# RWKV-style recurrence and two MoE layers on one core: prefix products by scans on chip, 64-row product pairs, and a new order

## The chip, the cores and the metric

The kernel runs on one core of one Trainium2 chip. The metric is the device time of one execution in microseconds. Of the kernel before there are three runs (1366.8, 1375.52 and 1378.17 us, median 1375.52) and one profiled execution.

## The reference

For each of 4 batches and 8 heads a 40x40 state is carried over 768 steps; then two MoE layers without routing follow (really two dense feed-forward layers of 3072 tokens, 320 -> 2048 -> 320):

```
for t in range(768):                       # per batch, head; all 40 wide
    y[t]  = r[t] @ state
    Sa    = state @ a[t]
    state = state * w[t] - outer(Sa, b[t])   # w in 0.85..0.95
    state = state + outer(v[t], k[t])
x = y as (3072 tokens, 320)
h = x @ w_in;  x = (h * sigmoid(h)) @ w_out          # layer 1
h = x @ w_in2; out = max(0.01*h, h) @ w_out2         # layer 2
```

The weights come as 64-bit floats and are turned into 32-bit ones on the chip.

## The kernel before, in words

The recurrence is cut into 12 chunks of 64 steps. A chunk c has two halves of 16 heads, and the program counts them as x = 0..23 (x = 2c + half). In a chunk everything is matrix products, after each step's keys and queries are scaled by the running product of w (P) or by its reciprocal (Q).

**Start.** `prefix(g)` (L626) computes P for a group of four chunks, in rows of steps: 14 products on `scratch`, a clamp, two reductions into `pmm`, eight reciprocals of 320 elements, and it writes P and Q to four DRAM tensors, as rows (`pd`, `qd`) and transposed (`ptd`, `qtd`). Group 0 is on VectorE, groups 1 and 2 multiply on GpSimd. In the same time 40 pieces of the first layer's weights are decoded (`w1_piece`, L883) in slots of `carved` and `scratch`.

**Attention.** `pre(x)` (L675) loads P and Q, forms SA = a*P, transposes K and b (`kr`), multiplies them by Q (`kbt`), and multiplies `kbt` with SA on TensorE in two groups of four 128x128x128 products (`bank<-sa,kbt`; two matmul records each). VectorE masks a part back into SA, ScalarE copies a part that goes to DRAM (`s2d`). `solve(c)` (L726) loads it back spread over 128 partitions (`ilm`), runs a 32-step substitution of 62 operations on GpSimd (`ilt`, `ily`), and writes `yd`. `chain(x)` (L753) loads that as `yt`, computes the states' part (`tv,sa`), two solves (`carved,yt` and `uv,s`), the state update (`uv,kb`), the product of uv with r (`carved,uvt`, two groups of four 128x128x128 products against RB, a block-diagonal copy of r), and the outputs (`carved` with TT, then `kb,carved`), which times P give `xt`, 128 tokens of layer-1 input. The ring `sa` has four buffers, and `pre` and `solve` of chunk c+1 are recorded ahead of the chains of chunk c.

**MoE.** Every two chains complete a block of 256 tokens, for which `moe_block` (L488) multiplies in the float32-rounded format with high and low parts, 16 steps f of 14 matmuls: eight of `xs` with the first weights and six of `gs` with the second. Between them ScalarE takes SiLU and VectorE the low part of `gs`. Blocks 0 to 10 of layer 1 run between attention work (phase 1). Block 11 and the 12 blocks of layer 2 run behind it (phase 2). In phase 1 the second layer's weights are decoded too, in 20 pieces, and kept in DRAM (`w2d`).

**What sets the order.** Every operation is recorded and then ordered by `Plan.run` (L242), a greedy list scheduler: at each step it takes, on the engine that can start first, the task with the lowest due time. The due times come from the table DUE (L339), one row for each kind of work with offsets for the first few uses; `cost` (L122) holds what it assumes of durations. It also hands out PSUM banks (four of group `t` for attention, two `h` and two `o` for the MoE). All recorded operations therefore show line L370 in the profile (L386 in the changed kernel). All transfers are issued by SyncE.

Of the kernel before, what the change touches and what calls it, by code (L numbers as in the profile page):

```python
# [58 lines left out]
class Plan:  # L59
# [5 lines left out]
    QUEUE, LAND = 800.0, 1350.0  # L65

    def __init__(self, nc, groups):
        self.nc, self.groups = nc, groups
        self.tasks, self.log, self.cur, self.done, self.since = [], {}, None, {}, 0.0
        self.busy = {k: [0.0] * len(v) for k, v in groups.items()}  # L70
        self.free = dict.fromkeys(self.HOP, 0.0)
        self.dma, self.port = 0.0, {"vector": 0.0, "gpsimd": 0.0}
        self.win, self.work, self.warm, self.mode = 0, {}, False, True
# [48 lines left out]
    def cost(eng, name, out, ins, kw):  # L122
# [4 lines left out]
        if eng == "sync":  # L127
            return 600.0
        if eng == "tensor":
            if name == "transpose":  # L130
                return 107.0
            m = 1
            for d in ins[0].shape[1:]:
                m *= d
            if ins[0].dtype == F32R:
                return max(n, 2 * m) / 2.4 + 13
            if out.start > 0:
                return 2 * m / 2.4
            return 4 * max(n, m) / 2.4 + 4
        if eng == "vector":  # L140
            fixed = 125 if psum else 69
            if name == "reciprocal":
                return fixed + 6 * n / 0.96
            if name == "scalar_tensor_tensor":
# [3 lines left out]
            if name in ("tensor_copy", "tensor_scalar", "memset") and not psum:  # L148
                return fixed + n / 1.92
            return fixed + n / 0.96  # L150
        if eng == "scalar":
            return (57 if psum else 94) + n / 1.2
# [8 lines left out]
    def record(self, engs, name, args, kw):  # L161
# [18 lines left out]
        if name != "memset":  # L180
            t.port = t.port or sum(not isinstance(x, Bank) for x in ins) > 1 or (
                not any(isinstance(x, Bank) for x in ins + [out]) and name in ("tensor_copy", "tensor_scalar", "tensor_tensor")
            )
        if engs == ("sync",):
            short = min(x.run for x in (Shape(out), Shape(ins[0])))
            t.lat = Shape(out).bytes / (360.0 if short >= 512 else 180.0)
# [55 lines left out]
    def run(self):  # L242
# [24 lines left out]
        while left:  # L267
            best = None
            for e, ts in avail.items():
                cand = []  # L270
                for t in ts:
# [15 lines left out]
                    if ok:  # L287
                        if t.port and e in self.port:
                            est = max(est, self.port["gpsimd" if e == "vector" else "vector"])
                        cand.append((est, t))  # L290
# [18 lines left out]
            if e == "sync":  # L309
                begin = max(end + self.QUEUE, self.dma)  # L310
                self.dma = begin + t.lat
                late = begin - end - self.QUEUE
            self.emit(t, e)
# [24 lines left out]
    W1 = 9.37  # L338
    DUE = {  # L339
        "first": ((), -100.0, 0.0),  # L340
        "w1": ((-8.4, -23.65), 36.91, 2.03),
        "load": ((-3.07, -14.35, -6.52, -6.22, -4.43), -1.98, 2.03),
        "pre": ((-6.91, -15.06, -11.45, -1.23, -9.35), -10.11, 6.63),
        "solve": ((-3.56, -4.67, -4.89, -5.93, -12.46), -13.61, 4.21),
        "v": ((), -1.31, 0),
        "rows": ((), 0.85, 0),
        "chain": ((-0.19, -2.2, -2.86, 0.46, -3.64), -1.49, 0.05),
        "moe": ((0.74, 0.32, -14.78), -0.59, 4.78),
        "prefix": ((17.19, -20.66, 22.32), 16.09, 13.34),
        "w2": ((), 10.7, 10.97),  # L350
# [9 lines left out]
    def emit(self, t, e):  # L360
# [8 lines left out]
        for name, args, kw in t.ops:  # L369
            getattr(eng, name)(*[real(x) for x in args], **{k: real(x) for k, x in kw.items()})  # L370
# [62 lines left out]
def attention_moe_kernel(  # L433
# [16 lines left out]
    pmm = const.tile([128, 2, 3], F32, name="pmm")  # L450
# [12 lines left out]
    VG = plan.on("vector", "gpsimd")  # L463
# [24 lines left out]
    def moe_block(W, layer, get_x, put, gs, xs, xo, turn):  # L488

        n = xs.shape[1]  # L490
        plan.window("moe", turn if layer == 1 else NB, 4 * turn + (4 if layer == 1 else 52), 106)
# [58 lines left out]
    with ExitStack() as c1:  # L550
# [9 lines left out]
        pa = many(1, [128, 8, E], "pa")  # L560
        rp = many(1, [128, 2, 8, E], "rp")
        pt = many(1, [128, 8, C + 1], "pt")
        qt = many(1, [128, 8, C], "qt")
        pc = many(4, [128, 8], "pc")
        kb = many(2, [128, 16, E], "kb")
        kr = many(2, [128, 8, 64], "kr")
        kbts = many(1, [128, 4, 2, C], "kbt")
        uv = many(1, [128, 16, E], "uv")
        tv = many(3, [128, 2, 8, E], "tv")
        sa = many(4, [128, 8, 2, 64], "sa")  # L570
        carved = one([128, 3, 2048], "carved")
        rbd = Ring([carved[:, 0, 0:1024].rearrange("p (v o t) -> p v o t", v=8, o=2)])
        s34s = Ring(carved[:, 0, 1024 + 512 * i : 1536 + 512 * i].rearrange("p (h t) -> p h t", h=8) for i in range(2))
        tt = [carved[:, 1, 640 * i : 640 * i + 640].rearrange("p (v o e) -> p v o e", v=8, o=2) for i in range(2)]
        tp = [carved[:, 2, 512 * i : 512 * i + 512].rearrange("p (v e) -> p v e", v=8) for i in range(2)]
        rr = Ring([carved[:, 2, 1024:1536].rearrange("p (v t) -> p v t", v=8)])
        uus = Ring([carved[:, 2, 1536:2048].rearrange("p (v o e) -> p v o e", v=4, o=2)])
        uvts = many(1, [128, 2, 4, 2, 64], "uvt")
        zts = Ring([carved[:, 1, 1280:1600].rearrange("p (v e) -> p v e", v=8)])
        s2s = one([128, 4, 16, 32], "s2")  # L580
        s2m = Ring(s2s[0:32, i] for i in range(4))
        s2rs = Ring(s2s[64:128, i, 0:8] for i in range(4))
        yt = many(2, [128, 8, 32], "yt")

        il_mm = one([128, 2, 2, 16, 32], "ilm")
        il_ys = many(2, [128, 2, 8, 32], "ily")
        il_0 = carved[:, 1, 1600:1856].rearrange("p (j t) -> p j t", j=8)
# [5 lines left out]
        wp, wt = scratch[:, 0 : (C + 1) * E], scratch[:, (C + 1) * E :]  # L593
# [8 lines left out]
        for t in sa + tv + qt + pt:  # L602
# [3 lines left out]
        for i in range(3):  # L606
            A.copy(xs[64:128, i, 1, 2, :], sa[1].rearrange("p v o t -> p (v o t)")[64:128, 0:128])
# [9 lines left out]
        il_00 = il_ys[0][:, 0]  # L617
        G.memset(il_00, 0.0)
        for base, fill in ((0, -1.0), (32, 0.0)):
            G.affine_select(  # L620
                out=il_00, in_=il_00, pattern=[[-128, 8], [32, 32]], compare_op=ALU.is_gt, fill=fill, base=base, channel_multiplier=-1
# [3 lines left out]

        def prefix(g):  # L626

            PV = V if g == 0 else G
            G.memset(wp[:, 0:E], 1.0)
            wr = w.rearrange("b h (c t) e -> c (b h) (t e)", t=C)  # L630
            for j in range(4):
                SY.dma_start(out=wp[32 * j : 32 * j + 32, E:], in_=wr[4 * g + j])
            wv = wp[:, E:].rearrange("p (a i e) -> p a i e", a=8, i=8)
            for i in range(1, 8):
                PV.tensor_tensor(out=wv[:, :, i, :], in0=wv[:, :, i - 1, :], in1=wv[:, :, i, :], op=ALU.mult)
            for n in range(1, 8):
                PV.tensor_tensor(
                    out=wv[:, n], in0=wv[:, n], in1=wv[:, n - 1, 7:8, :].broadcast_to([128, 8, E]), op=ALU.mult
                )
            V.tensor_scalar(wp, wp, P_MIN / 2, P_MAX * 2, op0=ALU.max, op1=ALU.min)  # L640

            room = il_mm.rearrange("p f x i t -> p (f x i t)") if g == 0 else wt
            n = 4 * (C + 1)
            rooms = itertools.cycle([room[:, n * i : n * i + n] for i in range(room.shape[1] // n)])

            def transposed(dst, x):
                for q in range(10):
                    z, qs = next(rooms)[:, : 4 * x.shape[2]].rearrange("p (e t) -> p e t", e=4), slice(4 * q, 4 * q + 4)
                    A.copy(z, x[:, qs])
                    SY.dma_start(  # L650
                        out=dst[4 * g : 4 * g + 4, :, qs].rearrange("c x e t -> (c x) (e t)"), in_=z.rearrange("p e t -> p (e t)")
                    )

            def rows(dst, x):
                for j in range(4):
                    SY.dma_start(
                        out=dst[4 * g + j].rearrange("t x e -> x t e"),
                        in_=x[32 * j : 32 * j + 32].rearrange("x (t e) -> x t e", e=E),
                    )

            transposed(ptd, wp.rearrange("p (t e) -> p e t", e=E))
            rows(pd, wp[:, : C * E])
            V.tensor_reduce(out=pmm[:, 0, g : g + 1], in_=wp, axis=AX.X, op=ALU.min)
            V.tensor_reduce(out=pmm[:, 1, g : g + 1], in_=wp, axis=AX.X, op=ALU.max)
            for i in range(8):
                V.reciprocal(wv[:, i], wv[:, i])
            transposed(qtd, wp[:, E:].rearrange("p (t e) -> p e t", e=E))
# [502 lines left out]
```

## Time and profile before

| | us |
|---|---|
| runs | 1366.8, 1375.52, 1378.17 |
| profiled execution, span | 1371.1 |
| PE busy | 1100.0 (80%) |
| DVE busy | 759.1 (55%) |
| ACT busy | 728.1 (53%) |
| POOL busy | 408.7 (30%) |
| first matmul of layer 1's block 0 | 211.8 |
| first matmul of blocks 1 to 5 | 294.0, 366.1, 448.4, 529.6, 604.3 |
| first matmul of blocks 6 to 10 | 684.4, 741.0, 807.0, 872.1, 918.5 |
| first matmul of block 11 (phase 2) | 968.1 |

The span is the profiled execution's on the chip's own clock; the runs' times are taken from outside, and the median stands 4.4 us over the span. The block starts cut the span into a start (0 to 212), eleven blocks with attention between (212 to 968) and phase 2 (968 to 1371). A TensorE busy share says nothing by itself: beside it stands the granted clock, and at half clock the same work is busy twice as long.

### The profile page before, as it was taken

What the parts mean: (1) busy time and instruction counts of PE and PEld (TensorE: products, weight loads), DVE (VectorE), ACT (ScalarE), POOL (GpSimd) and SP (SyncE); (2) the same over time, 40 slices, a digit from 0 to 9 for tenths busy, and PEclk for the clock granted to TensorE, in tenths of its full rate; (3) what the DMA queues carried; (4) which work ended last, traced back from release to release, by engine and by line L of the source; (5) the groups of instructions that cost most, each with busy time, mean ns of one, the idle gap of its engine ahead of it and who ended that gap; (6) DMA issues with size and microseconds to landing.
All of it is one profiled execution on the core that took longest, in us unless ns stands there. A gap on an engine that the chain in (4) does not pass through costs nothing.

```text
span 1371.1 us, 31938 instructions
## 1 busy us (share of the span) xinstructions
PE 1100.0 (80%) x12370; PEld 1041.4 (76%) x12370; DVE 759.1 (55%) x1498; ACT 728.1 (53%) x1863; POOL 408.7 (30%) x868
## 2 busy tenths in 40 slices
PE   1043166869896797779799888999799999999997
PEld 0042056869796686779798888899799999999997
DVE  8888863547335265326476655554564544445543
ACT  5445574546643465456466555665654444444443
POOL 4244825826033741625263444520000000000000
PEclk9985579889996997989899999999899999999999
DMA  8765347646546546746676755543520100000000
GB/s 208 168 171 149 108 116 154 146 127 115 127 109 155 125 110 137 164 104 153 159 188 159 169 153 127 131 109 89 170 65 22 26 24 21 20 21 25 16 13 20
DMA packets 325400, 149.82 MB, mean 109 GB/s; under 512 B 270712, under 2 KB 293752, under 8 KB 324856
## 3 DMA queue, kind: packets, MB, share of 16 engines
q1 hardware_dynamic: 325240, 147.70, 44.7%
q8 instruction: 99, 1.62, 0.5%
q14 instruction: 61, 0.50, 0.1%
HBM read 111.93 MB, written 35.71 MB: 108 GB/s over the span
## 4 chain that ended last, share of the span: by engine, by line
PE 47%; DMA 19%; POOL 9%; ACT 8%; DVE 6%; issue 5%; SPq 5%; ACTq 0%; POOLq 0%; DVEq 0%
PE bank L370 47%; SPq L370 5%; POOL ily L370 3%; POOL ilt L370 3%; DVE scratch L370 3%; DMA carved<-in_xr_dram 3%; ACT carved L370 2%; DMA ilm<-s2d 2%; POOL scratch L370 2%; DMA ptd<-scratch 2%; DMA w2d<-scratch 2%; DMA scratch<-in_moe_w_out_dram 1%; DMA kr<-in_xkb_dram 1%; DMA yd<-ily 1%; DMA qt<-qtd 1%
## 5 line engine op out<-in xcount | busy, mean ns | idle before, releaser
L370 PE MATMUL bank<-oh,gs 128*128 128x320 f32 x1344 | 363.4, 322 | 0.0
L370 PE MATMUL bank<-xs,ih 128*128 128x256 f32 x1536 | 307.8, 293 | 43.1 <-DVE gs L370 36.2
L370 PEld LDWEIGHTS bank<-xs,ih 128*128 128x128 f32 x1536 | 252.0, 196 | 48.7 <-DVE gs L370 40.4
L370 PEld LDWEIGHTS bank<-oh,gs 128*128 128x128 f32 x1344 | 245.7, 194 | 2.6 <-ACT xo L370 0.4
L370 POOL TENSOR_TENSOR ilt<-ily,ilm 128x120 f32<-128x120 f32 (+24 forms) x372 | 158.9, 427 | 238.6 <-DMA ilm<-s2d 186.1
L370 PE MATMUL bank<-xs,il 128*128 128x256 f32 x768 | 221.4, 288 | 0.0
L370 PE MATMUL bank<-ol,gs 128*128 128x320 f32 x672 | 211.8, 315 | 0.0
L370 DVE TENSOR_TENSOR gs<-bank,gs 128x256 fp32r<-128x256 f32 x192 | 80.2, 420 | 178.3 <-ACT gs L370 177.1
L370 POOL TENSOR_TENSOR ily<-ily,ilt 128x120 f32<-128x120 f32 (+24 forms) x372 | 160.8, 432 | 28.0
L370 PE MATMUL bank<-xs,i 128*128 128x256 f32 x768 | 157.8, 288 | 0.0
L370 PEld LDWEIGHTS bank<-xs,il 128*128 128x128 f32 x768 | 151.1, 197 | 0.0
L370 DVE TENSOR_TENSOR gt<-bank,gt 128x256 f32<-128x256 f32 x192 | 81.4, 424 | 108.6 <-ACT gt L370 108.5
L370 ACT ACTIVATE gt<-bank 128x256 f32<-128x256 f32 x192 | 73.8, 384 | 114.4 <-PE bank L370 113.5
L370 PEld LDWEIGHTS bank<-ol,gs 128*128 128x128 f32 x672 | 131.4, 196 | 0.0
L370 ACT ACTIVATE bank<-bank 128x256 f32<-128x256 f32 x192 | 70.8, 368 | 105.9 <-PE bank L370 104.7
L370 PEld LDWEIGHTS bank<-xs,i 128*128 128x128 f32 x768 | 123.1, 197 | 0.0
L370 PE MATMUL bank<-sa,kbt 128*128 128x128 f32 x384 | 64.3, 321 | 50.7 <-DVE kbt L370 44.6
L370 PEld LDWEIGHTS bank<-sa,kbt 128*128 128x128 f32 x384 | 57.2, 228 | 55.3 <-POOL kb L370 25.8
L370 PE MATMUL bank<-gs,onesr 128*1 128x256 f32 (+1 forms) x40 | 15.7, 404 | 99.5 <-ACT gs L370 99.5
L370 DVE TENSOR_TENSOR gs<-gt,gs 128x256 fp32r<-128x256 f32 x144 | 60.7, 422 | 47.4 <-ACT gs L370 45.3
L370 PEld LDWEIGHTS bank<-gs,onesr 128*1 128x1 f32 x40 | 3.4, 86 | 109.2 <-ACT gs L370 108.9
L370 ACT CAST gs<-gt 128x256 fp32r<-128x256 f32 x144 | 58.2, 405 | 49.8 <-DVE gt L370 49.5
(128 smaller groups left out, 1957.7 us busy)
## 6 DMA issues: line engine op xcount, KB each, us to landing
kr<-in_xkb_dram SPq DMA_DIRECT2D x48, 256.0 KB
ilm<-s2d SPq DMA_DIRECT2D x48, 256.0 KB
kb<-in_xkb_dram SPq DMA_DIRECT2D x24, 320.0 KB
rp<-qd SPq DMA_DIRECT2D x48, 160.0 KB
scratch<-in_moe_w_out_dram SPq DMA_DIRECT2D x8, 640.0 KB
scratch<-in_moe_w_in_dram SPq DMA_DIRECT2D x18, 256.0 KB
scratch<-in_moe_w_in_dram SPq DMA_DIRECT2D x8, 512.0 KB
pt<-ptd SPq DMA_DIRECT2D x48, 81.2 KB
```

The costliest lines, as they stand in the source:

```text
L370: getattr(eng, name)(*[real(x) for x in args], **{k: real(x) for k, x in kw.items()})
```

## The change

`prefix` and its four DRAM tensors go. A new function `scans(c)` loads w of one chunk, transposes it on TensorE and forms P by six scans per chunk straight in the transposed layout (`pw`). `pre` gets its row copy of P by four transposes back (`pa`), takes the reciprocal of 512 columns per x on VectorE, and makes K rows out of the scaled `kbt` by eight transposes (window "kt"). The products with SA, and those of uv with r, are done as sixteen 64-row products of 64 columns, rows 0-63 and 64-127 into two banks, in place of eight (two groups of four) 128-row ones of 128 columns: the block-diagonal copies RB and UU go. SA has three buffers for four, `scratch` two slots for three, a solve loads in two transfers for four and stores in one for eight. The planner gets a new table DUE, other durations and another model of transfers, and `pre(x+2)` is recorded ahead of each chain.

```diff
-    pd = dram.tile([NC, C, B * H, E], F32, name="pd")
-    qd = dram.tile([NC, C, B * H, E], F32, name="qd")
-    ptd = dram.tile([NC, B * H, E, C + 1], F32, name="ptd")
-    qtd = dram.tile([NC, B * H, E, C], F32, name="qtd")
+    VG, VA = plan.on("vector", "gpsimd"), plan.on("vector", "scalar")
-        sa = many(4, [128, 8, 2, 64], "sa")
+        sa = many(3, [128, 2, 8, 64], "sa")
-        scratch = one([128, 3 * 3 * DM], "scratch")
+        scratch = one([128, 2 * 3 * DM], "scratch")
+        def scans(c):
+            plan.window("scan", c, 4 * c, 14)
+            VG.memset(wr[:, :, E:], 1.0)
+            for bp in range(2):
+                SY.dma_start(
+                    out=wr[64 * bp : 64 * bp + 64, :, 0:E],
+                    in_=w[2 * bp : 2 * bp + 2, :, C * c : C * c + C, :].rearrange("b h t e -> t (b h) e"),
+                )
+            for vs in (range(0, 3), range(3, 6), range(6, 8)):
+                n, vo = len(vs), slice(vs.start, vs.stop)
+                ps = plan.bank("t", [128, 2, n * C + 1])
...
+                        T.transpose(ps[:, :, C * i + 1 : C * i + C + 1], flat(wr[:, h : h + 2]), ident)
+                V.tensor_copy(pcs[:, c, :, vo], ps[:, :, C::C])
+                V.memset(ps[:, :, 0 : n * C : C], 0.0)
+                for bp in range(2):
+                    V.tensor_tensor_scan(
+                        flat(pw[:, bp, vo]), ps[:, bp, 0 : n * C], flat(heads1[:, 0:n]), 0.0, op0=ALU.mult, op1=ALU.add
+                    )
+            V.tensor_tensor(out=pcs[:, c], in0=pcs[:, c], in1=pw[:, :, :, C - 1], op=ALU.mult)
+            for i, op in enumerate((ALU.min, ALU.max)):
+                V.tensor_reduce(out=pmm[:, i, c : c + 1], in_=pw.rearrange("p b v t -> p (b v t)"), axis=AX.X, op=op)
         def pre(x):
...
+                    T.transpose(both(ps[:, u]), flat(W[:, 2 * u : 2 * u + 2]), ident)
+            VA.copy(PA, ps.rearrange("p u o e -> p (u o) e")[:, :, 0:E])
+            V.reciprocal(at[:, :, 0 : C - 1], W[:, :, 1:])
+            V.reciprocal(at[:, :, C - 1], PC)
...
+            ps = [plan.bank("t", [128, 8, C]) for o in range(2)]
+            with plan.group():
+                for v in range(8):
+                    for o in range(2):
+                        q = slice(64 * o, 64 * o + 64)
+                        T.matmul(ps[o][:, v], flat(kbt[q, v]), SA[q, o, v % 4 * 2 + v // 4], start=True, stop=True)
...
+                plan.window("kt", x, 2 * x + b2, 5)
...
+                        T.transpose(ps[:, u].rearrange("p o e -> p (o e)"), flat(kbt[:, 4 * b2 + u]), ident)
+                VA.copy(K[:, 8 * b2 : 8 * b2 + 8], ps.rearrange("p u o e -> p (u o) e")[:, :, 0:E])
         def chain(x):
...
-                for u in range(4):
-                    T.transpose(ps[:, u], flat(UU[:, u]), ident)
-            A.copy(uvt[:, :, :, 0], ps.rearrange("p u b t -> p b u t"))
...
-                        T.matmul(ps[:, 2 * u : 2 * u + 2], flat(uvt[:, b2, u]), RB[:, 4 * b2 + u], start=True, stop=True)
+                for v in range(8):
+                    for o in range(2):
+                        q = slice(64 * o, 64 * o + 64)
+                        T.matmul(ps[o][:, v], flat(UVR[q, v, 0:2]), R[q, v], start=True, stop=True)
...
-        def ahead(c):
-            pre(2 * c)
-            pre(2 * c + 1)
-            solve(c)
         for x in range(NP):
-            if x % 2 == 0 and x + 2 < NP:
-                ahead(x // 2 + 1)
+            if x + 2 < NP:
+                pre(x + 2)
+            if x % 2 == 1 and x + 2 < NP:
+                solve(x // 2 + 1)
```

In the rows of order that follow, a name before the arrow is what is written, those behind it what is read; numbers after a name are the buffer's. `xs`, `ih`, `il`, `i` are the first MoE product's, `gs`, `oh`, `ol` the second's.

VectorE, at the start. Before, behind the first decoded pieces, the prefix products' reciprocals and those of the first chunk's Q (`qt`) lie ahead of the first `kbt`:

```order
L370 RECIPROCAL scratch<-scratch 128x320 x8
...
L370 RECIPROCAL qt_111<-pt_110 40x256
L370 TENSOR_TENSOR carved<-carved 128x256
L370 TENSOR_TENSOR ol_103<-carved,oh_102 128x320
L370 MEMSET carved 128x512
...
L370 TENSOR_TENSOR kbt_120<-bank_88,qt_111 128x512
L370 RECIPROCAL qt_111<-pt_110 40x256 x2
```

And now (a scan prints as SCALAR_TENSOR_TENSOR of `pw`):

```order
L386 COPY pcs<-bank_86 128x2x2
L386 MEMSET bank_86 128x2x2
L386 SCALAR_TENSOR_TENSOR pw<-bank_86,heads_111 128x128
...
L386 RECIPROCAL at<-pw 128x8x63
L386 TENSOR_TENSOR scratch<-scratch 128x320
L386 RECIPROCAL at<-pcs 128x8
L386 TENSOR_TENSOR kbt<-bank_87,at 128x512
L386 TENSOR_TENSOR ol_99<-scratch,oh_98 128x320
L386 TENSOR_TENSOR kbt<-bank_84,at 128x512
```

The first `kbt` stands at row 92 in place of 82, with two reciprocals (of 504 and 8 elements) ahead of it in place of eleven; each of the 24 x has such a pair now. The first `gs` of the MoE stands at row 304 (before: 280), and six `pre` stand ahead of it in place of five and a half.

TensorE, behind block 2 of layer 1, before: 50 rows of attention alone (ten of them shown) until block 3 begins at row 765.

```order
L370 MATMUL bank_85<-oh_102,gs_78 128x320
L370 MATMUL bank_91<-ident,kr_119 128x128 x4
L370 MATMUL bank_89<-carved,uvt_130 128x128 x4
L370 MATMUL bank_91<-sa_125,kbt_120 128x128 x4
L370 MATMUL bank_89<-ident,kr_118 128x128 x4
...
L370 MATMUL bank_89<-tv_122,sa_126 32x40 x16
L370 MATMUL bank_90<-sa_128,kbt_120 128x128 x4
L370 MATMUL bank_88<-ident,kr_119 128x128 x4
L370 MATMUL bank_86<-ident,xt_76 128x128 x2
L370 MATMUL bank_86<-ident,xt_76 64x128
L370 MATMUL bank_88<-sa_128,kbt_120 128x128 x4
...
L370 MATMUL bank_87<-xs_107,ih_99 128x256 x2
```

And now, in the middle of phase 1:

```order
L386 MATMUL bank_81<-oh_98,gs_75 128x320
L386 MATMUL bank_84<-uv_113,s_124 32x40 x16
L386 MATMUL bank_87<-sa_117,kbt 128x64
L386 MATMUL bank_85<-sa_117,kbt 128x64
...
L386 MATMUL bank_83<-xs_103,ih_95 128x256 x2
...
L386 MATMUL bank_83<-xs_103,i_97 128x256 x2
L386 MATMUL bank_86<-carved,yt_125 32x40 x16
L386 MATMUL bank_84<-tv_115,sa_118 64x40 x14
L386 MATMUL bank_84<-tv_115,sa_118 32x40 x4
L386 MATMUL bank_86<-uv_113,kb_122 40x40 x16
L386 MATMUL bank_80<-oh_98,gs_76 128x320
```

Pieces of attention stand between runs of 6 to 14 MoE matmuls, and the transposes of the next block's `xt` stand within the block before it, so that no stretch of attention alone separates blocks.

SyncE, at the end of phase 1. Before, five stores of decoded second-layer weights (`w2d`) stand behind the last `yt`, the last of them right ahead of the first loads of phase 2:

```order
L370 DMA yt_132<-yd 128x8x32
L370 DMA yt_133<-yd 128x8x32
...
L370 DMA w2d<-scratch 128x512
L370 DMA scratch<-in_moe_w_out_dram 128x2x640 x2
L370 DMA w2d<-scratch 128x640
L370 DMA x2d<-xo 128x320
L370 DMA w2d<-scratch 128x640
L370 DMA x2d<-xo 128x320
L370 DMA xt_10423<-x2d 128x320
```

And now:

```order
L386 DMA w2d<-scratch 128x640
L386 DMA uv_113<-in_xv_dram 64x1024 x2
...
L386 DMA yd<-ily_129 128x2x256
L386 DMA yt_125<-yd 128x8x32
L386 DMA yt_126<-yd 128x8x32
```

The last of them has moved ahead of the last solve's store. SyncE's program has 549 rows in place of 791.

## Rows read from the trace of the kernel before

**Rows 1.** Windows over the stages: length, busy us by engine, clock, DMA share, GB/s.
```profile
0.00:212.00 212.00, 64.82 (x775) 48.11 (x776) 173.16 (x326) 115.03 (x276) 94.13 (x175) 0.78 0.62 154
212.00:604.00 392.00, 315.83 (x4066) 294.41 (x4065) 178.89 (x297) 200.45 (x510) 165.17 (x368) 0.87 0.59 132
604.00:968.00 364.00, 325.20 (x4556) 305.69 (x4550) 206.10 (x391) 218.83 (x556) 149.38 (x325) 0.96 0.57 141
968.00:1371.00 403.00, 394.11 (x2986) 393.21 (x2986) 200.93 (x485) 193.76 (x522) 0.00 (x0) 0.99 0.13 35
...
395.00:449.00 54.00, 39.81 (x521) 35.72 (x520) 31.10 (x56) 22.97 (x59) 28.23 (x51) 0.78 0.60 145
```

**Rows 2.** Waits of PE, 212 to 604: total us, times, longest.
```profile
PE bank L370 <- DVE gs L370: 27.5, 10, 8.0
PE bank L370 <- DMA yt<-yd: 11.5, 4, 4.0
```

**Rows 3.** Timeline of PE behind block 2: start, duration, operation, idle before.
```profile
423.13 1.09 PE L370 MATMUL bank<-ident,carved 128*128 128x128 f32 x4 [4.75 <-DVE kbt L370]
...
448.38 0.48 PE L370 MATMUL bank<-xs,ih 128*128 128x256 f32 x2
```

**Rows 4.** Operations of DVE by shape: busy us, mean ns, idle before.
```profile
L370 DVE RECIPROCAL scratch<-scratch 128x320 f32<-128x320 f32 x24 | 50.3, 2127 | 4.6 <-DMA pd<-scratch 3.9 <-ACT scratch L370 0.6
L370 DVE RECIPROCAL qt<-pt 40x256 f32<-40x256 f32 x8 | 13.8, 1731 | 0.2
L370 DVE TENSOR_REDUCE pmm<-scratch 128x1 f32<-128x2600 f32 x6 | 17.0, 2847 | 0.0
...
L370 DVE SCALAR_TENSOR_TENSOR carved<-carved 128x256 uint32<-128x256 uint32 x8 | 3.3, 418 | 0.0
```

**Rows 5.** The chain that ended last, around a solve: start, us, what.
```profile
858.46 2.39 DMA s2d<-s
860.86 7.25 DMA ilm<-s2d
...
906.16 1.96 DMA yd<-ily
```

**Rows 6.** Timeline of PE at full clock: start, duration, operation (two records a product, transposes one).
```profile
401.72 0.60 PE L370 MATMUL bank<-ident,kr 128*128 128x128 f32 x4
402.25 0.36 PE L370 MATMUL bank<-carved 128*64 128x80 f32 x4
402.44 0.38 PE L370 MATMUL bank<-kb,carved 128*64 128x40 f32 x8
402.64 0.34 PE L370 MATMUL bank<-carved 128*64 128x80 f32 x4
...
404.98 0.77 PE L370 MATMUL bank<-tv,sa 128*32 128x40 f32 x32
405.68 0.76 PE L370 MATMUL bank<-carved,yt 32*32 32x40 f32 x32
406.37 0.77 PE L370 MATMUL bank<-tv,sa 128*32 128x40 f32 x32
...
853.75 1.05 PE L370 MATMUL bank<-sa,kbt 128*128 128x128 f32 x8
854.56 0.39 PE L370 MATMUL bank<-oh,gs 128*128 128x320 f32 x1
```

**Rows 7.** Weight loads of the products with SA (from the page).
```profile
L370 PEld LDWEIGHTS bank<-sa,kbt 128*128 128x128 f32 x384 | 57.2, 228 | 55.3 <-POOL kb L370 25.8
```

**Rows 8.** The page's group of POOL's solve steps, and their second half.
```profile
L370 POOL TENSOR_TENSOR ilt<-ily,ilm 128x120 f32<-128x120 f32 (+24 forms) x372 | 158.9, 427 | 238.6 <-DMA ilm<-s2d 186.1
L370 POOL TENSOR_TENSOR ily<-ily,ilt 128x120 f32<-128x120 f32 (+24 forms) x372 | 160.8, 432 | 28.0
```

**Rows 9.** The chain that ended last, across the end of phase 1: start, us, what.
```profile
952.24 5.03 DMA w2d<-scratch
...
963.21 2.17 DMA w2d<-scratch
965.90 2.21 DMA xt<-x2d
```

More of the change, by code (lines that the diff above doesn't have):

```diff
@@ L136, in cost @@
                 return max(n, 2 * m) / 2.4 + 13
+            if ins[0].shape[0] == 64 and m == 128:
+                return 60.0
             if out.start > 0:
@@ L151, in cost @@
         if eng == "scalar":
-            return (57 if psum else 94) + n / 1.2
+            return (57 if psum else 94) + n / 1.2 + (95 if out.shape[0] < 128 else 25)
         if name == "memset":
@@ L181, in record @@
             t.port = t.port or sum(not isinstance(x, Bank) for x in ins) > 1 or (
-                not any(isinstance(x, Bank) for x in ins + [out]) and name in ("tensor_copy", "tensor_scalar", "tensor_tensor")
+                not any(isinstance(x, Bank) for x in ins + [out]) and name in ("tensor_copy", "copy", "tensor_scalar", "tensor_tensor")
             )
         if engs == ("sync",):
-            short = min(x.run for x in (Shape(out), Shape(ins[0])))
-            t.lat = Shape(out).bytes / (360.0 if short >= 512 else 180.0)
+            a, b = Shape(out), Shape(ins[0])
+            rows = math.gcd(a.shape[0], b.shape[0])
+            k = max(i for i in range(1, 17) if rows % i == 0)
+            t.lat = max(a.bytes / k / 22.0, a.bytes / min(a.run, b.run) / k * 15.0)
         t.ops.append((name, args, kw))
@@ L571, in attention_moe_kernel @@
[L571 to L582, printed above, removed]
+        pa = many(3, [128, 8, E], "pa")
+        pw = one([128, 2, 8, C], "pw")
+        kr = one([128, 16, 64], "kr")
+        at = one([128, 8, C], "at")
@@ new lines, in attention_moe_kernel @@
+        kbt = one([128, 8, 2, C], "kbt")
+        wr = kbt.rearrange("p v b t -> p (v b) t")
+        heads1 = one([128, 3, C], "heads1")
+        pcs = one([128, NC, 2, 8], "pcs")
+        uv = many(1, [128, 16, 64], "uv")
+        tv = many(3, [128, 2, 8, E], "tv")
+        sa = many(3, [128, 2, 8, 64], "sa")
+        carved = one([128, 6144], "carved")
+        cuts = itertools.accumulate([0, 512, 512, 640, 640, 512, 512, 320, 256, 640, 64])
+        cut = [carved[:, i:j] for i, j in itertools.pairwise(cuts)]
@@ new lines, in attention_moe_kernel @@
+        s34s = [x.rearrange("p (v t) -> p v t", v=8) for x in cut[0:2]]
+        tt = [x.rearrange("p (v o e) -> p v o e", v=8, o=2) for x in cut[2:4]]
+        tp = [x.rearrange("p (v e) -> p v e", v=8) for x in cut[4:6]]
+        uvrs = many(1, [128, 8, 3, 64], "uvr")
+        zts = Ring([cut[6].rearrange("p (v e) -> p v e", v=8)])
+        kb = Ring([ap.tile([128, 16, E], F32, name=f"kb{i}") for i in range(2)] + [cut[8].rearrange("p (h e) -> p h e", h=16)])
+        s2s = one([128, 3, 16, 32], "s2")
@@ L624, in attention_moe_kernel @@
         A.copy(il_ys[1][:, 0], il_00)
[L626 to L667, printed above, removed]
-            rows(qd, wp[:, E:])
@@ L698, in pre @@
[L698 to L706 removed]
+            SY.dma_start(out=kr, in_=xkb[x])
@@ L873, in put1 @@
             return f
-        early = [st for i in range(3) for st in words(carved[:, i], plan.M1)]
+        early = words(carved, plan.M1)
         words1, words2 = words(scratch, plan.M1), words(scratch, plan.M2)
```

261 lines of the change are left out of this document (124 added, 137 removed).

## The prediction

> **What bounds the kernel now.** I read the windows over the three stages first [rows 1], because the busy shares of the whole span mix stages with different limits. In the start, 0 to 212, VectorE is busy for 173.16 us and TensorE for 64.82: VectorE's work and the waits in between set the time. In phase 2, 968 to 1371, TensorE is busy 394.11 of 403 us at a clock of 0.99, and the change touches nothing there: these 403 us stay. Between them lie 756 us in which TensorE should be the bound and is not. Busy time must be multiplied by the granted clock to be compared: 315.83 x 0.87 = 275 us of full-clock work stand in the 392 us of the early five blocks, and 325.20 x 0.96 = 312 in the 364 of the late six. That is 70% and 86% of what TensorE could do; phase 2 reaches 394.11 x 0.99 / 403 = 97%. So about 170 us of these 756 are lost to waiting and to the low clock, and two thirds of them early.
>
> The waits of TensorE and its timeline tell why. From 212 to 604 it waits longest on `gs` from VectorE, 27.5 us in 10 waits, then on `yt`, the solve's answer, 11.5 [rows 2]. Behind block 2 all the MoE's matmuls are used up, and from 395 to 449 there is attention alone: 39.81 busy us at a clock of 0.78 [rows 1], single waits of 4.75 us [rows 3], and block 3 begins only at 448.38. A chain of small operations that hands over between engines leaves TensorE idle; the clock falls, and what is left of it takes longer.
>
> **The start.** Gone ahead of the first `gs` are eight reciprocals of 2127 ns, eight of `qt` with 13.8 us, and two reductions of 2847 ns [rows 4]: 17.0 + 13.8 + 5.7 = 36.5. Added for three chunks, six x: a reciprocal of 512 columns at 2127 / 320 = 6.65 ns a column is 3.4 us, six of them 20.4; six reductions of 1024 at 2847 x 1024 / 2600 = 1.12 us are 6.7; 18 scans. No row shows a scan. Its nearest rows below are an ordinary two-input operation of 256 columns, 418 ns, and above the reciprocal's rate, 192 x 6.65 = 1.28 us [rows 4]; as it multiplies and adds like the former I take 0.42, so 7.6 us (23 at the other end). Sum 34.7: VectorE has as much to do as before. What can go is its idle time, 212 - 173 = 39 us, some of which waited for P and Q on their way through DRAM. I take half of that: layer 1 gets going at 195 (bounds 180 and 212).
>
> **TensorE's work in the 756 us.** It holds 275 + 312 = 587 us at full clock. Per x the change adds 16 transposes, four of which take 402.25 - 401.72 = 0.53 us [rows 6]: +2.1. The 18 products of `tv,sa` replace 32, of which 16 take 0.70: -0.6. Transposes of uv are eight half-height ones for four: +0.2. The disputed term is the pair products, 32 in place of 16. A full one costs (854.56 - 853.75) / 4 = 0.20 us. A 64-row one has half the rows and half the columns; no row shows that shape. Nearest below is the K-row product of 40 columns and 64 output rows, 0.20 / 4 = 0.05; above, the full one with 0.20, since the weights loaded are as wide (228 ns a load [rows 7]). I take the row nearest in columns, 80 columns to 64 output rows in alternating halves, 0.19 / 2 = 0.095 [rows 6]: 32 x 0.095 = 3.0 for 16 x 0.20 = 3.2, -0.2. Together +1.5 per x, and 22 x lie in these blocks: +33, so 620 us.
>
> [...] The rows show `tv,sa` (128*32) and `yt` (32*32) groups following each other at 0.70 and 0.69 us [rows 6], with no gap that stands out.
>
> **The order.** The attention-only stretches go: pieces of it now stand between runs of 6 to 14 MoE matmuls, and the next block's transposes stand within the running block. Then the early blocks have no reason to differ from the late ones, 86%, and the late ones lose some of their waits too; phase 2's 97% is the ceiling. I go a third of the way from the late rows to the ceiling, 89.5%, as a handed-over chain still runs beside: 620 / 0.895 = 693 us, 63 a block. The tail of stores and loads of the second layer's weights, from 952.24 to 968 [rows 9], has moved ahead, which may give up to 16 us; it is part of that percentage. VectorE has 385 us in the 756 [rows 1], 35 a block. The reciprocals (22 x 3.4 = 75), scans (66 x 0.42 = 28) and reductions (22 x 1.12 = 25) add 128, against 45 of the later groups' reciprocals and reductions (16 x 2.127 + 4 x 2.847 [rows 4]) that go, some 8 a block: 43 of 63, not the bound. ScalarE and SyncE lose work; I count nothing, since neither ended many waits.
>
> **Sum.** 195 + 693 + 403 = 1291 us of span, against the profiled execution's 1371. The median of the runs stands 4.4 above its span: 1295.
>
> **The rivals.**
> *The solve's loop sets the block.* `s2d` 2.39, `ilm` 7.25, the steps (158.9 + 160.8) / 12 = 26.6 on POOL [rows 8], `yd` 1.96 [rows 5], `yt` up to 4.0 [rows 2]: 42 us. Attention on TensorE is 587 / 11 = 53 less a block of MoE, 394 / 13 = 30, so 23, and 26 with the added 3. If three SA buffers for four let nothing of it overlap with the solve, a block takes 68: 195 + 748 + 403 + 4 = 1350. For it: waits on `yt`, one buffer less. Against it: `pre` is recorded two x ahead, and fewer transfers lie between. 0.14.
>
> *The reciprocal holds up `gs`.* An operation of 3.4 us stands in VectorE's queue ahead of the next `gs`, the wait that was largest. If half of it stops TensorE at each of 22, that is 37 us: 1332. Against it: reciprocals and `gs` are apart in the order by planned time. 0.08.
>
> *Pair products cost as much as full ones.* At 0.20 each the 32 are 6.4 us per x, 3.4 more, 22 x 3.4 / 0.895 = 84: 1380, within 1% of before. For it: a load of as many weight columns. 0.08.
>
> *The order gains nothing (slower).* The early loss may come from hand-overs between engines, which the new order does not shorten; then the efficiency stays at the whole stretch's 587 / 756 = 78%, and TensorE's added 33 cost 43: 1371 - 17 + 43 + 4 = 1401. It decides once a block takes over 71 us ((1389 - 4 - 195 - 403) / 11). For it: more and smaller pieces, 24 more long operations on VectorE. Against it: late blocks already run at 60.7 us with the same hand-overs [rows 1]. 0.07.
>
> That the change does not do what it says is out: the DRAM tensors are gone from the order's rows.
>
> **How the numbers follow.** The forecast has 0.60; 0.03 is left for better than it. Its own range: with pair products at 0.05 (-32 us of work), 95% and a start of 180 it is 180 + 588 / 0.95 + 403 + 4 = 1206; with 86%, scans at their upper price (57 us more on VectorE, of which I let a third through, 19) and a start of 205 it is 205 + 721 + 19 + 403 + 4 = 1352. Both ends need everything at once, so I cut the lower to 1225 and let the upper stand at 1358, which takes in the solve and the reciprocal; the pair products at full price and the order that gains nothing stay out. One per cent, about what a measurement of this kernel can tell, is 1362 to 1389. Faster by more: the forecast, the solve, the reciprocal and what is below, less what of them runs over, 0.82. Within: the pair products and that overrun, 0.10. Slower: the order, and pair products above the full price, 0.08.
>
> **What would show it.** Right: dense MoE from about 195; block starts 63 us apart, early as late; a clock of 0.95 or more from the second block on; no stretch of tens of microseconds without MoE matmuls; 403 for phase 2. The pair products are read from the timeline: 16 in 1.5 us, or 0.8, or 3.2. A scan's mean shows in VectorE's groups. Wrong: blocks of 68 with TensorE waiting on `yt` (the solve), waits on `gs` behind a reciprocal, or early blocks still near 78 us with a low clock (the order). What would break the forecast most is the percentage of 89.5, the one number chosen and not read: each point of it is 8 us.

## The result, and the profile after

The changed kernel takes 1302.5 us (median of 4 runs, 1296.6 to 1304.2) against 1371.2 us: a ratio of 0.948, 95% interval 0.943 to 0.953. The forecast was 1295 us with a range of 1225 to 1358. The profiled execution has a span of 1294.8 us; it is the fastest of the four runs.

The page of the changed kernel, busy time by engine and the chain that ended last:

```profile
PE 1136.7 (88%) x12946; PEld 1071.6 (83%) x12946; DVE 828.5 (64%) x1678; ACT 657.6 (51%) x1690; POOL 368.5 (28%) x792
...
PE 42%; ACT 2%; DVE 2%; issue 1%; DMA 1%; DVEq 0%; ACTq 0%
```

The second line cannot be set beside that of the kernel before as it stands: its shares add up to 48%, because the chain could be followed back only to 660 us. From there to phase 2 (660 to 892) TensorE has 69.5% of the chain. In the kernel before it has 39.9% of it from 660 to 968, with transfers and the solve's operations on GpSimd among the rest. The windows, cut where block 1 and phase 2 begin (length, busy us of PE, PEld, DVE, ACT, POOL, clock, DMA share, GB/s):

```profile
0.00:289.00 289.00, 164.67 (x1743) 139.16 (x1744) 214.38 (x440) 138.72 (x336) 106.96 (x224) 0.72 0.46 116
289.00:892.00 603.00, 579.38 (x8222) 540.82 (x8221) 412.52 (x758) 325.90 (x835) 261.54 (x568) 0.99 0.44 114
892.00:1294.00 402.00, 392.61 (x2983) 391.60 (x2983) 201.64 (x482) 193.00 (x521) 0.00 (x0) 0.99 0.13 35
```

The same middle stretch of the kernel before, from its block 1 to its phase 2:

```profile
294.00:968.00 674.00, 575.96 (x7793) 538.99 (x7792) 350.22 (x629) 376.74 (x960) 272.14 (x608) 0.92 0.57 135
```

Read the second row against this one: 71 us shorter, with nearly the same busy time of TensorE at a higher granted clock, which means more work (579 x 0.99 = 574 us at full clock against 576 x 0.92 = 530). Busy time multiplied by clock is an estimate. What it rests on is that eight records of full products are busy for 1.05 us at full clock [rows 6, at 853.75] and for 2.05 in the kernel before's start, where the clock is 0.50, 1.95 times as long:

```profile
112.91 2.05 PE L370 MATMUL bank<-sa,kbt 128*128 128x128 f32 x8 [5.44 <-DVE kbt L370]
```

TensorE did not get less to do; it stopped waiting, 23.6 us idle for 98. The start gave 5 us (block 1 at 288.6 for 294.0), phase 2 nothing. So the gain is in the ten blocks: 60.3 us each for 67.4. TensorE's waits in those blocks (total, times, longest), two lines of the kernel before (294 to 968) and then three of the changed kernel (289 to 892):

```profile
PE bank L370 <- DVE gs L370: 32.1, 16, 8.0
PE bank L370 <- DMA yt<-yd: 12.5, 6, 4.0
PE bank L386 <- DVE gs L386: 15.5, 16, 2.3
PE bank L386 <- ACT s L386: 2.7, 7, 0.9
PE bank L386 <- ACT xs L386: 2.3, 1, 2.3
```

`yt`, the solve's answer, is no longer among them. What replaced [rows 4], VectorE's new operations (busy us, mean ns, idle before):

```profile
L386 DVE RECIPROCAL at<-pw 128x504 f32<-128x504 f32 x24 | 79.0, 3291 | 0.2
L386 DVE TENSOR_REDUCE pmm<-pw 128x1 f32<-128x1024 f32 x24 | 28.7, 1207 | 0.1
L386 DVE TENSOR_TENSOR_SCAN pw<-bank,heads 128x192 f32<-128x192 f32 x48 | 24.2, 540 | 0.2
L386 DVE TENSOR_TENSOR_SCAN pw<-bank,heads 128x128 f32<-128x128 f32 x24 | 8.8, 406 | 0.1
```

And the pair products on TensorE's timeline, which answer to [rows 6]:

```profile
405.87 0.31 PE L386 MATMUL bank<-oh,gs 128*128 128x320 f32 x1
406.11 2.00 PE L386 MATMUL bank<-sa,kbt 64*128 64x64 f32 x32
408.04 0.51 PE L386 MATMUL bank<-xs,ih 128*128 128x256 f32 x2
```

Sixteen of them take 408.04 - 406.11 = 1.93 us from start to start, 0.12 each. The two groups of four full products that they replace took 0.81 to 0.99 each at full clock: 0.81 in [rows 6] at 853.75, and 0.89 here, since the next row of [rows 6] starts at 401.72:

```profile
400.83 1.06 PE L370 MATMUL bank<-sa,kbt 128*128 128x128 f32 x8
```

### The profile page after: what moved, and what is told of

It reads as the page before. It is cut to its first block, busy times and chain, and to the rows that moved or that the text cites. A ratio compares the mean times of both kernels' runs of the same rounds, so it can differ in the third digit from the quotient of the medians.

```text
span 1294.8 us, 32095 instructions
## 1 busy us (share of the span) xinstructions
PE 1136.7 (88%) x12946; PEld 1071.6 (83%) x12946; DVE 828.5 (64%) x1678; ACT 657.6 (51%) x1690; POOL 368.5 (28%) x792
## 5 line engine op out<-in xcount | busy, mean ns | idle before, releaser
L386 PE MATMUL bank<-oh,gs 128*128 128x320 f32 x1344 | 354.7, 316 | 0.4 <-DVE gs L386 0.4
L386 PEld LDWEIGHTS bank<-xs,ih 128*128 128x128 f32 x1536 | 245.0, 191 | 30.0 <-DVE gs L386 22.9
L386 PEld LDWEIGHTS bank<-oh,gs 128*128 128x128 f32 x1344 | 238.3, 189 | 3.4 <-DVE gs L386 0.9
L386 PE MATMUL bank<-ol,gs 128*128 128x320 f32 x672 | 207.8, 309 | 0.0
L386 PEld LDWEIGHTS bank<-xs,il 128*128 128x128 f32 x768 | 147.8, 192 | 0.0
L386 PEld LDWEIGHTS bank<-ol,gs 128*128 128x128 f32 x672 | 127.6, 190 | 0.0
L386 ACT COPY carved<-bank 32x320 f32<-32x320 f32 (+1 forms) x184 | 65.2, 354 | 59.2 <-PE bank L386 57.3
L386 PE MATMUL bank<-ident,kbt 128*128 128x128 f32 x288 | 50.5, 309 | 41.0 <-DVE kbt L386 30.4
L386 ACT ACTIVATE s<-bank 32x256 f32<-32x256 f32 x96 | 58.8, 613 | 53.7 <-PE bank L386 28.8
L386 DVE RECIPROCAL at<-pw 128x504 f32<-128x504 f32 x24 | 79.0, 3291 | 0.2
```

## The experiments

Every kernel was timed beside the kernel before. The table gives what the trace of one execution shows of the three stages, and the ratio of the median times to before's.

| kernel | block 1 begins | a block, mean of 1 to 10 | phase 2 begins | ratio (95%) |
|---|---|---|---|---|
| before | 294.0 | 67.4 | 968.1 | 1 |
| changed | 288.6 | 60.3 | 891.6 | 0.948 (0.943-0.953) |
| e1 pair products twice | 317.1 | 67.3 | 990.4 | 1.014 (1.011-1.018) |
| e2 128-row products | 298.9 | 64.2 | 941.4 | 0.975 (0.969-0.980) |
| e3 no reciprocal | 281.4 | 59.5 | 876.4 | 0.929 (0.926-0.933) |
| e4 old table | 274.5 | 74.3 | 1017.8 | 1.031 (1.028-1.034) |
| e5 new table on before | 318.8 | 75.7 | 1075.4 | 1.073 (1.070-1.077) |
| e6 18 early pieces | 270.7 | 73.5 | 1005.5 | 1.031 (1.028-1.034) |
| e7 three slots | 258.8 | 69.4 | 952.4 | 0.983 (0.981-0.985) |
| e8 longer solve, replanned | 285.1 | 77.3 | 1057.8 | 1.066 (1.063-1.068) |
| e9 longer solve, same order | 299.3 | 73.0 | 1029.0 | 1.041 (1.035-1.048) |
| e10 before, searched table | 332.8 | 58.9 | 921.4 | 0.963 (0.959-0.967) |
| e11 18 early, searched table | 264.6 | 64.1 | 905.2 | 0.953 (0.950-0.956) |
| e12 shorter solve, same order | 288.5 | 60.5 | 893.1 | 0.947 (0.944-0.951) |

**e1, pair products twice** (in both groups; the planner's price of one is halved, which keeps the order):

```diff
-                for v in range(8):
+                for v in 2 * list(range(8)):
```

> The changed kernel with both groups of sixteen 64-row products issued twice (48 groups more). Theory: TensorE is the bound in the blocks, and a group costs what its timeline shows, 1.93 us from start to start, some 0.2 of it the change of shape. The second issue then adds 1.7 to 1.9 us; of the 48 groups about 38 lie in the dense blocks (+65 to 72 us) and the rest in the start, which waits for other things (0 to 18 us): 1367 to 1392 us. Rival: the blocks are set by the solve's loop or by VectorE, and TensorE's extra work goes into its idle time: under 1335. Rival: pair products are nearly free, 0.05 each: 1302 + 30 to 38.

Measured 1396.5 us, 94 more. A doubled group on the timeline:

```profile
467.49 3.79 PE L386 MATMUL bank<-sa,kbt 64*128 64x64 f32 x64
471.21 0.51 PE L386 MATMUL bank<-xs,ih 128*128 128x256 f32 x2
```

3.72 for 1.93: the second sixteen add 1.79 us, 0.112 a product, and the remaining 0.14 of a group lies at its ends: in the changed kernel's group at 406.11 the second pair of records starts 0.160 us after the first and the next product 0.201 after the last pair, where the pairs between stand 0.112 apart. In the ten blocks stand 37 of the 48 groups; they are 67.8 us longer in all, and the blocks 70.3: every microsecond put on TensorE there is paid in full. The start grew by 28, more than expected: its chain runs through TensorE too, and a doubled group takes up to nearly twice as long there, 7.09 us for 3.79 (in the changed kernel's start a single group at 138.91, at a clock of 0.50, takes 3.61 us from start to start for 1.93):

```profile
149.94 7.09 PE L386 MATMUL bank<-sa,kbt 64*128 64x64 f32 x64
```

The start's eleven groups are 32.6 us longer in all. Both rivals are out.

**e2, the products of uv with r over 128 rows:**

```diff
-                        T.matmul(ps[o][:, v], flat(UVR[q, v, 0:2]), R[q, v], start=True, stop=True)
+                        T.matmul(ps[o][:, v], flat(UVR[:, v, 0:2]), R[:, v], start=True, stop=True)
```

> The changed kernel with the sixteen products of uv with r taken over all 128 rows in place of 64 (two heads are mixed, so the outputs of the recurrence within a chunk are not the reference's), in the same order. Theory: the two 64-row halves overlap, so 128-row products cost the 0.20 us of the full ones before: a group of 3.2 in place of 1.93 us, 24 times, of which 19 to 24 on the path: 1326 to 1333 us. Rival: a 64-column product costs the same at either height: within 5 us of 1302. Rival: the change of shape is what costs (0.1 us at each end): 1292 to 1300.

Measured 1342.0, 39 more than the changed kernel and above the 1326 to 1333 expected, with this group:

```profile
466.21 3.68 PE L386 MATMUL bank<-uvr 128*128 128x64 f32 x32
469.70 0.39 PE L386 MATMUL bank<-oh,gs 128*128 128x320 f32 x1
```

3.49 us for sixteen, 0.22 each in place of the 0.20 expected, as much as a full product of 128 columns (0.20 to 0.25): half the columns save nothing here. At 64 rows two products run in the time of one, 0.112 us each for 0.22, and side by side: in the trace of the changed kernel the records of the two halves start 7 ns apart, one such pair every 112 ns; here a single record takes 3.49 / 32 = 0.109 us (two records make a product in both). Both rivals are out.

**e3, a copy in place of the reciprocal,** at the planner's old price, so in the same order (some of the final flags' operations apart):

```diff
-            V.reciprocal(at[:, :, 0 : C - 1], W[:, :, 1:])
+            V.tensor_copy(at[:, :, 0 : C - 1], W[:, :, 1:])
```

> The changed kernel with a copy of the same 504 columns in place of each reciprocal (left out: the division), the planner's price kept. VectorE loses 24 x about 2.9 us = 70 us. Theory: reciprocals lie beside other work in the blocks, where TensorE waits for gs only 15.5 us in all; what goes is a part of that and some of the start: 1280 to 1300 us. Rival: each holds up gs by half its length (37 us) and the start as well: under 1270.

Measured 1279.3, 23 less by the medians, of 70 us of VectorE work; by the spans 15 less, 7 in the start and 8 in the ten blocks. So the two reciprocals of a block hold TensorE up by 0.8 us, not by half their length of 3.3 us each.

**e4, the old due times on the changed kernel** (the whole table DUE and W1 of the kernel before; for scans and K-row transposes rows of my own):

```diff
-        "moe": ((68.54, 3.57, 5.19, 6.37, 7.13, -2.22), -2.54, 8.93),
+        "moe": ((0.74, 0.32, -14.78), -0.59, 4.78),
...
+        "scan": ((), -12.0, 2.03),
+        "kt": ((), -8.0, 6.63),
```

> The changed kernel with the due times of the kernel before (for scans and for the transposes of K rows, rows like those of pre). Theory: the order gave most of the gain, 67.4 to 60.3 us a block; with the old due times blocks go back to 66 or 68 us: 1360 to 1385 us. Rival: the gain is from what left the path (transfers of P and Q, copies), and the greedy order finds it with any table: 1300 to 1320.

Measured 1419: slower than the kernel before. From block 1 to phase 2, and in a stretch of attention alone between blocks 2 and 3 (windows as above):

```profile
275.00:1018.00 743.00, 659.48 (x8315) 612.61 (x8313) 430.91 (x774) 335.65 (x849) 259.04 (x568) 0.86 0.37 96
...
371.00:441.00 70.00, 51.27 (x647) 44.56 (x646) 47.83 (x77) 22.71 (x54) 30.73 (x67) 0.61 0.45 113
```

All the change's operations are there, and these 70 us without a MoE matmul, at a clock of 0.61, are the picture of [rows 3] again; they make block 2 104 us long. The rows for scans and transposes were my choice, so the 1419 are no measure of the old table as such; that the greedy order finds the gain with any table is out.

**e5, the new due times on the kernel before** (table, W1 and recording order of the change; the prefix row kept; the planner's prices stayed those of the kernel before, against what the expectation says):

```diff
-        "moe": ((0.74, 0.32, -14.78), -0.59, 4.78),
+        "moe": ((68.54, 3.57, 5.19, 6.37, 7.13, -2.22), -2.54, 8.93),
...
-            if x % 2 == 0 and x + 2 < NP:
-                ahead(x // 2 + 1)
+            if x + 2 < NP:
+                pre(x + 2)
```

> The kernel before with the change's due times, planner's prices and recording order, and nothing else of the change (prefix products still through DRAM, full products, four SA buffers). Theory: the order carries most of the gain wherever it is put: blocks without attention-only stretches, 61 to 63 us each in place of 67.4, so 1371 - 45 to 65: 1305 to 1330 us. Rival: a due table fits only the operations that it was made for (the old one made the changed kernel slower than before): 1365 us or more.

Measured 1475, blocks of 75.7: a table fits the operations for which it was made, and nothing else. Whether before's operations admit a good order was open still; e10 asks that.

**e6, 18 of the 40 weight pieces in the early slots:**

```diff
-    EARLY, M1, M2 = 12, 1, 2
+    EARLY, M1, M2 = 18, 1, 2
```

> The changed kernel with 18 in place of 12 of the 40 first-layer weight pieces decoded in the six early slots, so that 22 in place of 28 go through the two slots of scratch. Theory: the start (block 1 at 288.6 us, the last weights split at 237.7) is bound by the decoding through two slots, where the kernel before had three and was done at 201.9: the last split 20 to 35 us sooner, block 1 and the whole 15 to 35 us: 1267 to 1288 us. Rival: the start is bound by the attention's first chunks, which now wait for the early slots too: 1300 to 1320.

Measured 1414, outside both expectations. The last weights were split at 193.0 (changed: 237.7) and block 1 began 18 us sooner, as the theory had it; but the blocks went to 73.5 us, since the planner, given other tasks, made another order.

**e7, three slots in `scratch`,** with two `pa` and two solve sources:

```diff
-        scratch = one([128, 2 * 3 * DM], "scratch")
+        scratch = one([128, 3 * 3 * DM], "scratch")
-        pa = many(3, [128, 8, E], "pa")
+        pa = many(2, [128, 8, E], "pa")
-        s2s = one([128, 3, 16, 32], "s2")
+        s2s = one([128, 2, 16, 32], "s2")
```

> The changed kernel with three decoding slots in scratch, as before, for which the rings of pa and of the solve's sources go from three to two buffers. Theory as for the 18 early pieces: last split near 200 us, and 1270 to 1288 us if the smaller rings cost nothing in the blocks. Rival: the start is bound by attention or VectorE: 1295 to 1310, or slower where the rings bind.

Measured 1349.8. The test is flawed, and the kernel does not compute the same: `pre(x+2)` is recorded ahead of `chain(x)`, so with two buffers the chain reads what `pre(x+2)` wrote there, and has to wait for it. Its start alone can be read: the last weights at 173, block 1 at 258.8.

**e8, a longer solve, replanned:** the first operation of each solve step is recorded twice.

```diff
+                for _ in range(2):
+                    G.tensor_tensor(
+                        out=t, in0=il_y[:, :, :J, i : i + 1].broadcast_to([128, 2, J, n]),
```

> The changed kernel with the first of the two operations of each solve step issued twice, 31 x 0.43 = 13 us more on POOL per chunk. Theory: the solve's loop (42 us and what TensorE does in between) has some 10 us to spare in a block of 60: 1302 to 1340. Rival: the loop sets the block already: eleven times 13, 1430 to 1445.

Measured 1462.5, more than the rival. But the order was another one again, so this says nothing on the loop. e9 holds the order.

**e9, a longer solve in the same order** (`emit` issues the operation twice; the planner does not know):

```diff
+            slow = e == "gpsimd" and "out" in kw and "ilt" in str(real(kw["out"]).tensor.name)
+            for _ in range(1 + slow):
```

> The changed kernel in exactly its own order on every engine, with the first operation of each solve step run twice: 31 x 0.43 = 13 us more per chunk on POOL. In the earlier run with the same extra work the planner knew of it and made another order, so that its 1462 us say nothing on the loop. Theory: in the tuned order the solve ends some us ahead of its use (TensorE waits for yt once, 4.5 us, in the whole run), so 13 us more are partly covered: 1310 to 1370. Rival: no room at all, 11 x 13: 1440 or more. Rival: room for all of it: within 8 us of 1302.

Measured 1435.9, 133 more: about the size of the rival without any room. TensorE's waits for `yt` in the whole run, one of these stops, and the window from block 1 to phase 2:

```profile
PE bank L388 <- DMA yt<-yd: 52.5, 9, 11.8
```
```profile
448.75 1.27 PE L388 MATMUL bank<-carved,yt 32*32 32x40 f32 x32 [6.83 <-DMA yt<-yd]
```
```profile
299.00:1029.00 730.00, 631.65 (x8243) 590.82 (x8237) 411.85 (x758) 327.60 (x835) 378.52 (x847) 0.88 0.37 94
```

Of the 127 us that this window is longer, 75 are idle time of TensorE (43.5 of it waits for `yt`, where the changed kernel has none), and 52 are longer busy time at the lower clock, 0.88 for 0.99. It looks like a loop that sets the block. e12 was made to tell that from an order that is just in time.

**e12, a shorter solve in the same order:**

```diff
+                if self.steps % 62 >= 40:
+                    continue
```

> The changed kernel in its own order, with the last 11 of the 31 solve steps left out (so the answers of the solve are not the reference's): about 9 us less per chunk on POOL. 13 us more had cost 133 us, 11 to 12 per chunk. Theory: TensorE, 96% busy in the blocks, is the bound, and the order is just in time: a longer solve delays everything behind its yt in TensorE's queue, a shorter one gives nothing in the blocks and a few us in the start: 1290 to 1305. Rival: the solve's loop sets the blocks: eleven times 9 less, 1205 to 1225.

Measured 1299.2; blocks of 60.5. By GpSimd's busy time a solve is 8.4 us shorter here, which gives nothing, and was 13.5 longer in e9, which cost 12.7 a block. The loop does not set the block. TensorE does, busy for 579 of the changed kernel's 603 us, and the order asks for `yt` just when it comes: the order of the queue is fixed, so a late answer stops the MoE matmuls behind it as well (in e9 TensorE stood idle for 6.83 us ahead of the `yt` products at 448.75).

**e10, the kernel before with a searched table:** none of the change's operations, its planner (prices and transfer model) and recording order, and due times found by a random search over the planner's own end time.

```diff
-        "moe": ((0.74, 0.32, -14.78), -0.59, 4.78),
+        "moe": ((-7.37, 12.43, -162.52, 45.48, 608.62, 124.72, -19.68, -3.34,), -14.88, 24.25),
...
```

> The kernel before (prefix products through DRAM, full products, four SA buffers, every operation as it was) with the change's planner and a table of due times that was searched anew for it, as the change's table was for the change. Theory: most of the gain is the order, since per block TensorE's own work did not get less (a group of sixteen pair products 1.93 us for two groups of four at 0.8 to 0.9, transposes added): blocks of 61 to 64 us and 1300 to 1335 us in all. Rival: what left the path (transfers, reciprocals in bulk, copies) is what made the dense blocks possible: 1350 us or more.

Measured 1326.1, 49 us of the change's 69. Its windows, start and blocks:

```profile
0.00:333.00 333.00, 156.81 (x1965) 130.25 (x1966) 231.50 (x403) 172.61 (x418) 158.75 (x331) 0.74 0.65 150
333.00:921.00 588.00, 541.18 (x7423) 509.17 (x7422) 325.13 (x606) 359.63 (x924) 247.06 (x543) 0.97 0.61 145
```

Its blocks are shorter than the changed kernel's, 58.9 us, because TensorE has less to do there (525 us at full clock for 574). Their density lies between the two: 525 / 588 = 89% of what TensorE could do, 79% before (530 / 674), 95% in the changed kernel. What it lacks is the start: 332.8 us to block 1, 44 behind the change. So most of the density needs no scans; it needs an order.

**e11, 18 early pieces with a searched table:**

```diff
-    EARLY, M1, M2 = 12, 1, 2
+    EARLY, M1, M2 = 18, 1, 2
-        "moe": ((68.54, 3.57, 5.19, 6.37, 7.13, -2.22), -2.54, 8.93),
+        "moe": ((356.82, 530.19, 647.1, 596.38, 1159.11, 1244.82, 619.95, 922.97,), -298.52, 418.25),
...
```

> The changed kernel with 18 early weight pieces and a table of due times searched anew for it. With the change's table 18 early pieces brought the last weights 45 us and block 1 18 us forward, and the blocks fell apart. Theory: with an order that fits, block 1 begins at 260 to 275 us and the blocks stay at 60 to 62: 1275 to 1295. Rival: the search finds no order as good as the one tuned on the chip: 1305 to 1340.

Measured 1310.2, ratio 0.953 beside 0.948: no better than the change. The start gained 24 us (block 1 at 264.6), the blocks lost 38 (64.1 each). The search, which knows only the planner's prices, found no block order as good as the change's. No version was found that beats the changed kernel and computes the same.

## Why the prediction was right, step by step

**The order, 89.5% of TensorE's time: right, and too low.** The stretches of attention alone went, early blocks run like late ones, the clock is 0.99, as forecast. The blocks reach 574 / 603 = 95%. At 89.5% these ten would have taken 38 us more. e10 shows that an order alone takes the old operations from 79% to 89%, and e4 that the new operations without a fitting order gain nothing. Whether the last six points come from the operations or from a better search is not shown. The tail of stores, for which up to 16 us stood in the percentage, was a small part: in the last 16 us ahead of phase 2 TensorE was idle for 6.9 us and is for 2.9.

**TensorE's added work: 33 us forecast, 54 measured.** At full clock phase 1 holds 165 x 0.72 + 574 = 692 us; before, 65 x 0.78 for the first 212 us and then the 587 of the prediction, 638. The 54 are for all 24 x; for these the forecast's 1.5 per x makes 36. The term of the pair products was sized too low: 0.095 taken, 0.121 with the ends of a group (32 x 0.026 x 24 = 20 us). They saved nothing against the full products that they replaced, 1.93 for 1.6 to 2.0, and e1 shows that they are paid. Those full ones were taken at 0.80 a group and took up to 0.99, so that not all of the 20 us is net and a part of the excess stays unexplained. The two errors pull against each other in the blocks: 57.4 us of work for the 56.4 forecast, at 95% in place of 89.5%, make 60.3 us for 63.

**The start: wrong.** The step was "layer 1 gets going at 195", half of VectorE's idle time. The first MoE matmul did come at 179.9, but the block ran densely only from 244.6, and block 1, due at 195 + 63 = 258, began at 288.6. VectorE's sum was right as far as it went (36.5 and 34.7 us; scans 0.54 and 0.41 for 0.42): up to 245 us VectorE is busy for 176, and in the kernel before, up to 212, for 173. Its idle time, which was to be halved, grew from 39 to 69 us. What I left out is the removal of a decoding slot: with two for three, the last first-layer weights were split at 237.7 us, and before at 201.9, although the DRAM round trip was gone. e6 and e7 move that split forward, and block 1 follows by 18 and 30 us. But the slots are not all of it: e4, with two slots and the old due times, has its last split at 215.2 and block 1 at 274.5, and e10, with three, has them at 191.2 and 332.8. How much is the slots and how much the order stays open. From the first matmul of block 0 to block 1 of the changed kernel:

```profile
180.00:245.00 65.00, 41.55 (x552) 36.58 (x551) 45.71 (x88) 30.63 (x73) 14.88 (x36) 0.56 0.39 106
245.00:289.00 44.00, 40.60 (x400) 38.08 (x399) 38.00 (x66) 19.30 (x51) 21.93 (x43) 1.00 0.48 119
```

From 245 TensorE is as good as full; the forecast did not have the 65 us ahead of it, at a clock of 0.56, in which only 24 of block 0's 224 matmuls are done.

**The sum: in part luck.** Block 1 came 31 us later than forecast, the ten blocks took 603 us for 630, 27 less, and phase 2 the 403 forecast. Two errors of opposite sign leave a span of 1294.8 for 1291. The 4.4 us from span to median did not hold either: the median stands 7.7 above the profiled span, because that execution was the fastest of the four; each run is 1.8 above its own span.

**The rivals.** *The solve's loop*: rejected by e12; but the solve has no room in this order either, as e9 shows with what each late microsecond costs. *The reciprocal*: there, at 8 us in the ten blocks in place of 37 in eleven (with the start 15 by the spans, 23 by the medians). *Pair products at full price*: e2 shows what they would have cost with all 128 rows, 0.22 us each; at 64 they run two at a time, 0.112 each. *The order gains nothing*: rejected; yet a wrong table turns the same change into e4.

What the change's operations themselves gave is at best the difference between e10 and it: 24 us by the medians and 31 by the spans, of which the start is 44 us shorter and the ten blocks 1.4 us longer each. The two orders were not searched alike, so a part of it may be the search; that is left open.

## What to carry to other kernels

Where a list scheduler writes the order, an edit is measured together with the luck of its new order, and that can be worth more than the edit: here 9% between two tables on the same operations (e4, two of whose rows were mine, and the change). Before the gain is put down to new instructions, search the order for the old kernel too, and test a suspected wait with the order held, once longer and once shorter. An in-order queue that asks for a result just in time charged a delay almost in full here (12.7 us for 13.5) and gave nothing for an earlier answer.

## What the runs showed of the hardware

A scan costs (540 - 406) / 64 = 2.1 ns an element on VectorE here. Ordinary two-input operations from PSUM take (682 - 486) / 192 = 1.0, by the means of `kbt` (512 columns, 682 ns) and of `xt` (320, 486 ns). So an element of a scan took twice the time of theirs.

Two operations that now permute what they write take longer. The changed kernel permutes the solve's sources while it writes them (ScalarE) and SA (VectorE); the same 256 elements took 373 ns before and 613 now, 512 of SA 740 before and 1128 now:

```profile
L370 ACT ACTIVATE s<-bank 32x256 f32<-32x256 f32 x96 | 35.8, 373 | 35.2 <-DVE sa L370 18.6 <-PE bank L370 15.6
L386 ACT ACTIVATE s<-bank 32x256 f32<-32x256 f32 x96 | 58.8, 613 | 53.7 <-PE bank L386 28.8 <-DVE sa L386 23.6
```
```profile
L370 DVE TENSOR_TENSOR sa<-sa,pt 40x512 f32<-40x512 f32 x36 | 26.7, 740 | 24.5 <-DMA sa<-in_xa_dram 12.8 <-DMA pt<-ptd 11.3
L386 DVE TENSOR_TENSOR sa<-at,pw 64x512 f32<-64x512 f32 x37 | 41.7, 1128 | 0.4
```

No run here separates the permuted order from the other differences of these operations (partitions, sources, reads in permuted order too).
